# Feeding the second stage earlier: piecewise hand-over of a buffer, twelve row blocks ahead instead of ten, four steps instead of six

## The chip, the cores and the metric

The kernel runs on one core of a Trainium2 chip. The metric is the device time of one execution in microseconds (us), lower is better. The core has five instruction streams that are ordered among each other only by semaphores: PE (matrix multiply, with its weight loads shown as PEld), ACT (activations and copies), DVE (vector work), POOL (vector work without access to the accumulators) and SP, which here issues all the DMAs in one queue.

## What is computed

Two layers follow each other. Layer A is an attention with a recurrent memory: the 2048 rows are cut into 64 segments of 32 rows, and each segment attends to itself and to 8 memory rows that the segment before has produced. So the 64 segments run strictly one after the other. Layer B is a gMLP that mixes all rows, so that its mixing can only begin when the last segment is done.

```python
for s in range(n_seg):                      # layer A, on layernorm(x)
    h = concat([mem, xs[s]])
    q, k, v = (einsum('btd,dhe->bhte', h, W) for W in (Wq, Wk, Wv))
    p = softmax(where(mask, q @ k.T * scale, -1e9))
    o = einsum('bhte,hed->btd', p @ v, Wo)
    mem = o[:, :M]
    outs.append(o[:, M:])
h = x + concat(outs)
...
z  = gelu(layernorm(h) @ w_in)              # layer B, w_in is 512 x 1792
z1 = z[..., :896]
z2 = layernorm(z[..., 896:])
g  = einsum('ts,bsf->btf', w_sp, z2) + b_sp # 2048 x 2048 mixing of the rows
out = h + (z1 * g) @ w_out
```

## The kernel before

All instructions are emitted in program order by hand; each engine runs its own in that order, and a small emitter turns reads and writes of named buffers into semaphore waits (`Emitter.add`, L55). A wait of an instruction holds everything behind it on the same engine.

**The loop over 64 segments** (L916 to L1066). In each segment PE computes Q and K (`QK`, matmul L500), the scores (`S_half`, L538 and L544), V (`V_half`, L591), the column sums of the softmax (`sm_sums`, L559 and L564), the weighted values (`PV_half`, L608 and L614) and the output projection (`Wo`, L641). Between the sums and `PV_half` PE would have to wait for ACT, DVE and POOL to finish the softmax (DVE L579 is its last step for the second half of the heads). This place, called the gap below, is filled with work that doesn't depend on the segment: first with batched work of layer A, one group in each of segments 1 to 47 (`gx`, for example `qkx_mm`, L414, 16 matmuls of 128x128), and then with the first matrix product of layer B for rows that are already final, here called z2 sums (`z2_narrow`, L751). A z2 sum of one row block of 128 rows and one half of 896 columns is 16 narrow matmuls, 4 for each of 4 pieces of the inner dimension; the narrow form (32 stationary columns, four beside each other) keeps the array in the form that the loop uses. A whole group of 16 goes into the gap by `z2_group`. A second supply, `pour`, adds single atoms of 4 narrow matmuls: one in each gap, and one more behind `Wo` in every fourth segment, called the end slot. The atoms are batched V columns (L433) first, and z2 sums after segment 48. The sums are copied out (DVE L759, ACT L761) and stored in DRAM as z2p (L762). In this way 10 of the 16 row blocks (`NP = 10`, L256) have their sums before the loop ends: 15 groups in segments 49 to 63 and 5 from atoms.

**The buffers.** The batched Q and K columns of the memory rows, QTx, lie in two buffers, each for 16 segments; the first half of a buffer holds Q for the 16 segments one after the other, the second half K. At segment s POOL copies its Q part (`qx_copy`, L523), and the matmul L544 reads its K part. The first buffer serves segments 32 to 47 and is free as a whole after them. Then, at segment 47, one DMA loads the second half of w_in into it (`w_in2`, L1059, 896 KB), and one DMA transpose a segment brings the normalised rows of blocks 0 to 7 (`xn2T_dma`, L730; blocks 8 to 10 by L743 into another buffer). The second buffer is free after segment 63; then follow the first half of w_in (`w_in1`, L971) and the transposes of blocks 8 to 13. DMA transposes of w_sp (`wT_piece`, L783 and L784) go through the same queue in every other segment. `z2_back` (L909) brings the stored sums back to the core: blocks 0 to 6 at segment 63, blocks 7 to 9 behind the loop, and the 8 pieces of the transposed w_sp follow them (`load_wT`, L905).

**The second stage** (from L1155). For the row blocks whose sums aren't there yet, 10 to 15, there are six steps k = 0 to 5. Each step has the two z2 sums of its block on PE (`z2_mm`, 4 matmuls L1099 each, then the gelu out of the accumulator, ACT L1102), the gelu of two blocks from DRAM (`z2_gelu`, ACT L1162), the normalisation of these three (`z2_norm`, DVE L1113 and L1115, POOL L1117 and L1119; `z2_apply`, DVE L1124), four groups of z1 (`z1_group`, PE L1131 and ACT L1134), and from k = 2 on the mixing of blocks that are ready into five accumulators (`mix0`, 5 matmuls L1138 for each block). z2 sums, z1 groups and the transposes of the last blocks (`xn2T_pe`, PE L1179, copied by DVE L1094; block 15 at k = 3) take turns on three accumulator banks (`zbank`), so that a matmul waits until the copy out of the third last user of the banks is done. Behind the steps come the remaining z1 groups, the rest of the first mixing, and the other 23 mixings with the output product (L1232).

Of the kernel before, what the change touches and what calls it, by code (L numbers as in the profile page):

```python
# [169 lines left out]
def fast_path(nc, st, keep, A_x, A_mem0, A_Wq, A_Wk, A_Wv, A_Wo, A_seg_len, B_w_in, B_w_sp, B_b_sp, B_w_out, out):  # L170
# [15 lines left out]
    CK = 16  # L186
# [536 lines left out]
    WH = DC * FH  # L723
    w_in2 = region(4 * WSZ, WH).rearrange("p (dc f) -> p dc f", dc=DC)
    w_in1 = region(4 * WSZ + QX, WH).rearrange("p (dc f) -> p dc f", dc=DC)
    xts = [region(4 * WSZ + i * QX + WH, 8 * D).rearrange("p (r dc t) -> p r dc t", r=8, dc=DC) for i in range(2)]
    winr = B_w_in.rearrange("(dc p) f -> p dc f", p=128)

    def xn2T_dma(rb, after):
        sp(lambda e: e.dma_start_transpose(out=xts[rb // 8][:, rb % 8, :, :], in_=xn2_d[rb]), reads=[("xn2d", rb)], writes=[("xn2T", rb)],  # L730
           after=after)
# [4 lines left out]
    def xT2(rb):  # L736
        return xts[rb // 8][:, rb % 8, :, :]

    def xT2z(rb):
        return (hTe[:, rb - 8, :, :], ("xT2e", rb)) if 8 <= rb <= 10 else (xT2(rb), ("xn2T", rb))  # L740

    def xT2e_dma(rb):
        sp(lambda e: e.dma_start_transpose(out=hTe[:, rb - 8, :, :], in_=xn2_d[rb]), reads=[("xn2d", rb)],  # L743
           writes=[("hTe", rb - 8), ("xT2e", rb)])

    def z2_narrow(rb, hf, bank, dcs=range(DC)):
        t, tok = xT2z(rb)
        for dc in dcs:
            for c in range(4):
                q = slice(32 * c, 32 * c + 32)  # L750
                pe(lambda e, dc=dc, q=q, c=c: e.matmul(ps[q, bank, 0:HF], lhsT=t[:, dc, q], rhs=w_in2[:, dc, hf * HF:(hf + 1) * HF],  # L751
                                                       start=(dc == 0), stop=(dc == DC - 1), tile_position=(0, 32 * c)),
                   reads=["w_in2", tok], writes=[PB(bank)])

# [158 lines left out]
    lastop = {}  # L913
    em.mark_const("w_in2")
    zx = [(rb, hf) for rb in range(NP) for hf in range(2)]
    qx_copy(0)  # L916
    for s in range(NSEG):
# [40 lines left out]
        S_half(s, 1)  # L958
        lastop["s"] = em.by_eng["pe"][-1]
        sm_exp(1)  # L960
# [9 lines left out]
        if s == NSEG - 1:  # L970
            sp(lambda e: e.dma_start(w_in1, winr[:, :, 0:FH]), writes=["w_in1"], after=[lastop["s"], lastop["x"]])  # L971
            xn2T_dma(11, [lastop["s"], lastop["x"]])
            z2_back(0, 7, lastop["v"])
        if s + 1 < NSEG:
            qx_copy(s + 1)
            lastop["x"] = em.by_eng["pool"][-1]
        sm_norm(0, pool)
        V_evac(1, "dve")
        sm_norm(1, dve)
        if s == 0:  # L980
# [73 lines left out]
        if j4 == 1 and rb >= 2:  # L1054
            xn2_apply(rb - 2, rb % 2)
            xn2_store(rb - 2, rb % 2)
        if s == 3 * CK - 1:
            free0 = [lastop["s"], px]
            sp(lambda e: e.dma_start(w_in2, winr[:, :, FH:F]), writes=["w_in2"], after=free0)  # L1059
# [17 lines left out]
    NTB = S // TB  # L1077
    em.mark_const("w_in1", "w_out")

# [16 lines left out]
    def z2_mm(rb, hf, bank):  # L1096
        t, tok = xT2z(rb)
        for dc in range(DC):
            pe(lambda e, dc=dc: e.matmul(ps[:, bank, 0:HF], lhsT=t[:, dc, :], rhs=w_in2[:, dc, hf * HF:(hf + 1) * HF],  # L1099
                                         start=(dc == 0), stop=(dc == DC - 1)),  # L1100
               reads=["w_in2", tok], writes=[PB(bank)])
        act(lambda e: e.activation(out=z2[:, rb, hf * HF:(hf + 1) * HF], in_=ps[:, bank, 0:HF], func=ACT.Gelu_apprx_tanh),  # L1102
            reads=[PB(bank)], writes=[("z2", rb, hf)], after=[lastV])

    st2 = sb("st2", [128, 4, 2, 6], F32)
    mv2 = sb("mv2", [128, 4, 2], F32)
    rs2 = sb("rs2", [128, 4], F32)
    nslot = {}

    def z2_norm(rb):  # L1110
        j = nslot[rb] = len(nslot) % 4
        for hf in range(2):
            dve(lambda e, hf=hf: e.bn_stats(out=st2[:, j, hf, :], in_=z2[:, rb, hf * HF:(hf + 1) * HF]), reads=[("z2", rb, hf)],  # L1113
                writes=[("st2", j, hf)])
        dve(lambda e: e.bn_aggr(out=mv2[:, j, :], in_=st2[:, j, :, :].rearrange("p a b -> p (a b)")),  # L1115
            reads=[("st2", j, 0), ("st2", j, 1)], writes=[("mv2", j)])
# [11 lines left out]
    def z1_group(tb, fb, bank):  # L1128
        r0 = 4 * tb
        for dc in range(DC):  # L1130
            pe(lambda e, dc=dc: e.matmul(ps[:, bank, 0:TB], lhsT=w_in1[:, dc, fb * 128:(fb + 1) * 128],  # L1131
                                         rhs=xts[r0 // 8][:, r0 % 8:r0 % 8 + 4, dc, :], start=(dc == 0), stop=(dc == DC - 1)),
               reads=["w_in1"] + [("xn2T", r) for r in range(r0, r0 + 4)], writes=[PB(bank)])
        act(lambda e: e.activation(out=z1T[:, fb, tb * TB:(tb + 1) * TB], in_=ps[:, bank, 0:TB], func=ACT.Gelu_apprx_tanh),  # L1134
# [49 lines left out]
    for k, rb in enumerate(range(NP, RB)):  # L1184
# [853 lines left out]
```

## Time and profile before

| | |
|---|---|
| median of 3 runs | 865.96 us (865.92 to 867.2) |
| the profiled execution, its own time | 866.2 us |
| span of the profiled execution | 864.4 us, so 1.8 us lie around it |
| granted PE clock, mean | 0.999 |
| segment loop | to 700.5 us, where the first L1099 starts |
| second stage up to the first mixing | 700.5 to 719.4 us |
| narrow z2 sums in the loop (L751) | 320 matmuls |
| z2 sums in the second stage (L1099) | 48 matmuls |
| reads of z2p | 1568 KB landed after 9.1 us, 672 KB after 4.4 us |

A line of a timeline shows the start in us from the start of the span, the duration, the engine, the line of the kernel, the operation with what it writes and reads, how many instructions were merged (x16), and in brackets how long the engine was idle before it and what released it. "issue" stands for idle time in which nothing that the profile shows was waited for. SPq is the SP queue issuing a DMA.

### The profile page before, as it was taken

Reading aid. Unit: us, or ns where it says so; the run is one execution under the profiler, and the core shown is the slowest. Engines: PE = TensorE matmul, PEld = TensorE weight load, DVE = VectorE, ACT = ScalarE, POOL = GpSimd, SP = SyncE. Lnnn points to the kernel's source line nnn. Section 1 sums busy time; section 2 is a strip of 40 time slices with the busy share of each in tenths; the row PEclk is TensorE's granted clock in tenths of the full one; section 3 lists DMA queues with packets and bytes.
Section 4 is the critical chain, followed back from the end, with each engine's and each line's share of the span. In section 5 each row is a group of like instructions: output and inputs, shape, how many; then the busy total and the mean of one; then the engine's idle time right before and its main releaser. Section 6 shows DMA issues by size and latency. Waiting matters only on the chain.

```text
span 864.4 us, 45375 instructions
## 1 busy us (share of the span) xinstructions
PE 844.7 (98%) x20839; PEld 476.3 (55%) x20849; DVE 526.8 (61%) x1191; ACT 420.9 (49%) x1085; POOL 158.1 (18%) x404
## 2 busy tenths in 40 slices
PE   6999999999999999999999999899999999999997
PEld 5755555655555655555565555455555544444443
DVE  3455676666666666666767666566666658363443
ACT  2445565555555555555555556455555566400000
POOL 5111122222111212121212121112212114100000
PEclk9999999999999999999999999999999999999999
DMA  9962221313202123121212121623232299032101
GB/s 324 378 216 61 65 60 52 68 31 86 59 25 74 41 59 62 32 65 46 62 37 62 38 60 45 110 70 80 74 64 63 67 241 345 10 109 98 38 13 39
DMA packets 105189, 76.20 MB, mean 88 GB/s; under 512 B 64024, under 2 KB 90528, under 8 KB 104992
## 3 DMA queue, kind: packets, MB, share of 16 engines
q1 hardware_dynamic: 104992, 73.24, 30.8%
q8 instruction: 165, 2.70, 1.4%
q14 instruction: 32, 0.26, 0.1%
HBM read 41.69 MB, written 20.91 MB: 72 GB/s over the span
## 4 chain that ended last, share of the span: by engine, by line
PE 94%; DVE 2%; DMA 1%; SPq 1%; issue 1%; POOL 0%; ACT 0%; DVEq 0%; POOLq 0%
PE f_ps L500 26%; PE f_ps L641 14%; PE f_ps L591 13%; PE f_ps L1138 11%; PE f_ps L414 6%; PE f_ps L692 4%; PE f_ps L1232 3%; PE f_ps L608 2%; PE f_ps L433 2%; PE f_ps L538 2%; PE f_ps L1131 2%; PE f_ps L751 2%; DMA f_arena<-in_A_Wk_dram 1%; PE f_ps L559 1%; DVE f_st L1113 1%; PE f_ps L614 1%
## 5 line engine op out<-in xcount | busy, mean ns | idle before, releaser
L500 PE MATMUL f_ps<-f_arena,f_hT 128*32 128x512 bf16 x4096 | 241.3, 380 | 2.2 <-issue 1.9
L507 ACT ACTIVATE f_Tst<-f_ps 128x512 bf16<-128x512 f32 x256 | 145.9, 596 | 80.5 <-PE f_ps L500 80.3
L500 PEld LDWEIGHTS f_ps<-f_arena,f_hT 128*32 128x32 bf16 x4096 | 94.9, 96 | 104.7 <-ACT f_hT L670 32.5
L591 PE MATMUL f_ps<-f_arena,f_hT 128*32 128x512 bf16 x2048 | 132.9, 378 | 0.0
L641 PE MATMUL f_ps<-f_arena,f_cT 128*32 128x256 bf16 x4096 | 128.6, 273 | 1.1 <-ACT f_cT L627 0.5
L641 PEld LDWEIGHTS f_ps<-f_arena,f_cT 128*32 128x32 bf16 x4096 | 98.2, 96 | 33.6 <-ACT f_cT L627 30.2
L513 DVE STREAM_TRANSPOSE f_QT<-f_Tst 128x256 uint32<-128x256 uint32 x128 | 57.0, 446 | 83.1 <-ACT f_Tst L507 83.1
L600 DVE CAST f_V_sb<-f_ps 128x512 bf16<-128x512 f32 x128 | 88.4, 691 | 29.6 <-PE f_ps L591 29.6
L1138 PE MATMUL f_ps<-f_arena 128*128 128x512 bf16 x448 | 99.6, 379 | 0.0
L523 POOL COPY f_QT<-f_arena 128x256 bf16<-128x256 bf16 x64 | 30.5, 476 | 314.1 <-PE f_ps L544 314.0
L627 ACT ACTIVATE f_cT<-f_ps 128x320 bf16<-128x320 f32 x128 | 49.0, 435 | 56.0 <-PE f_ps L614 56.0
L629 DVE TENSOR_SCALAR f_cT<-f_ps 128x320 bf16<-128x320 f32 x128 | 56.9, 486 | 31.5 <-PE f_ps L614 31.5
L1138 PEld LDWEIGHTS f_ps<-f_arena 128*128 128x128 bf16 x448 | 43.8, 98 | 52.6
L414 PE MATMUL f_ps<-f_hTe,f_arena 128*128 128x128 bf16 x1024 | 66.8, 222 | 2.6 <-DMA f_arena<-in_A_Wq_dram 1.8
L658 DVE CAST f_part<-f_ps 128x256 bf16<-128x256 f32 x64 | 27.2, 425 | 66.0 <-PE f_ps L641 66.0
L414 PEld LDWEIGHTS f_ps<-f_hTe,f_arena 128*128 128x128 bf16 x1024 | 58.9, 99 | 11.7 <-issue 9.6
L591 PEld LDWEIGHTS f_ps<-f_arena,f_hT 128*32 128x32 bf16 x2048 | 45.9, 95 | 27.3 <-issue 0.4
L516 DVE STREAM_TRANSPOSE f_KT<-f_Tst 128x256 uint32<-128x256 uint32 x128 | 55.4, 433 | 8.0
L571 ACT ACTIVATE f_R_sb<-f_ps 128x160 f32<-128x160 f32 x128 | 38.8, 303 | 42.0 <-PE f_ps L564 42.0
L1144 DVE TENSOR_TENSOR f_arena<-f_ps,f_arena 128x512 f32<-128x512 f32 x28 | 19.3, 690 | 60.7 <-PE f_ps L1138 60.7
L670 ACT ACTIVATE f_hT<-f_ps 128x16 bf16<-128x16 f32 x126 | 23.1, 183 | 55.2 <-PE f_ps L665 54.7
L528 DVE CAST f_ps<-f_mask 128x224 f32<-128x224 bf16 x128 | 47.0, 367 | 0.0
(121 smaller groups left out, 1099.8 us busy)
## 6 DMA issues: line engine op xcount, KB each, us to landing
wT_d<-f_wst SPq DMA_DIRECT2D x32, 256.0 KB, 2.4
f_arena<-wT_d SPq DMA_DIRECT2D x32, 256.0 KB, 4.8
f_arena<-in_A_Wq_dram SPq DMA_DIRECT2D x4, 1024.0 KB, 9.0
f_arena<-in_A_Wk_dram SPq DMA_DIRECT2D x4, 1024.0 KB, 14.7
f_arena<-in_A_Wv_dram SPq DMA_DIRECT2D x4, 1024.0 KB, 15.0
f_arena<-in_A_Wo_dram SPq DMA_DIRECT2D x8, 512.0 KB, 9.7
f_Vx<-vext_d SPq DMA_DIRECT2D x63, 64.0 KB, 2.8
vext_d<-f_Vs SPq DMA_DIRECT2D x24, 128.0 KB, 2.1
```

Of the source, the lines that this page charges most:

```text
L414: pe(lambda e, h=h, dc=dc, hh=hh: e.matmul(ps[:, bank, hh * 128:(hh + 1) * 128], lhsT=ws[:, dc, h * DH:(h + 1) * DH], rhs=hTe[:, ck % 3, d ...
L500: pe(lambda e, dc=dc, c=c, rhs=rhs: e.matmul(ps[32 * c:32 * c + 32, bank, :], lhsT=hT[:, sl, dc, :], rhs=rhs, start=(dc == 0), stop=(dc == ...
L507: act(lambda e: e.activation(out=Tst[:, tb, :].rearrange("p (hp i r) -> p hp i r", i=32, r=2), in_=ps[:, bank, :].rearrange("p (hp r i) -> ...
L513: dve(lambda e: e.transpose(out=dst, in_=src), reads=[("T", tb)], writes=[("QT", b)])
L516: dve(lambda e: e.transpose(out=dst, in_=src), reads=[("T", tb)], writes=[("KT", b)])
L528: dve(lambda e: e.tensor_copy(out=ps[:, bank, 0:224], in_=mask[:, :]), reads=["mask"], writes=[PB(bank)])
L591: pe(lambda e, dc=dc, c=c, c0=c0: e.matmul(ps[32 * c:32 * c + 32, bank, :], lhsT=hT[:, sl, dc, :], rhs=w_v[:, dc, c0:c0 + 512], start=(dc ...
L600: dve(lambda e: e.tensor_copy(out=V_sb[:, b, :], in_=ps[:, bank, :]), reads=[PB(bank)], writes=[("V", b)])
L627: act(lambda e: e.activation(out=dst, in_=src, func=ACT.Copy, scale=UNSC), reads=[PB(PVB[c])], writes=[("cT", c)])
L629: dve(lambda e: e.tensor_scalar(out=dst, in0=src, scalar1=UNSC, scalar2=None, op0=ALU.mult), reads=[PB(PVB[c])], writes=[("cT", c)])
L641: pe(lambda e, h=h, g=g, i=i, b=b, c=c: e.matmul(ps[32 * g:32 * g + 32, bank, 0:d1 - d0], lhsT=cTh[:, i, 8:40], rhs=w_o[:, h, d0:d1], star ...
L1138: pe(lambda e: e.matmul(ps[:, bank, 0:TB], lhsT=z2[:, sc, fb * 128:(fb + 1) * 128], rhs=wTb[tb % 2][:, :, sc, :], start=(n == 0), stop=(n ...
```

## The change

QTx's first buffer is handed over piece by piece: each of the four pieces of w_in2 lies in the part of segments that have passed, and so does each row block. The pieces of w_in2 are loaded two at segment 36 and two at segment 39, row blocks 0 to 7 are transposed in at segments 40 to 47 (in the order 0, 4, 1, 5, 2, 6, 3, 7), block 8 at segment 49, 9 to 13 at segments 50, 52, 54, 58 and 62, and w_in1's pieces come at segments 53, 55, 59 and 61, all of them in the second buffer's parts as these become free. With that, z2 sums can be poured from segment 42 on (`Z0`), a whole group goes into the gap from segment 48 on, and in odd segments after 48 `pour` may put two atoms into the gap. The sums of 12 row blocks are made in the loop, 384 narrow matmuls. Laid out by segment, the gaps of 42 to 47 get 4 narrow matmuls more than before (beside 16 of L414), the gap of 48 gets 20 where it had none, those of 49, 51, 53, 57, 59 and 61 get 24 instead of 20, those of 62 and 63 16 instead of 20; the end slots of 44 and 48 get 4, that of 62 none.

The second stage has four steps, for blocks 12 to 15, each with the gelu and the norm of three blocks from DRAM instead of two; the transpose of block 15 moves from k = 3 to k = 2. The line that reads blocks 7 to 11 back stands twice in the new text, one right behind the other, and both issue a DMA. Both write the same buffers, so the second one waits in the SP queue until the first has landed.

```diff
-    NP = 10
+    NP = 12
...
-    w_in2 = region(4 * WSZ, WH).rearrange("p (dc f) -> p dc f", dc=DC)
+    QH = QX // 2
+    w_in2 = [region(4 * WSZ + (dc // 2) * QH + (dc % 2) * FH, FH) for dc in range(DC)]
...
-    xts = [region(4 * WSZ + i * QX + WH, 8 * D).rearrange("p (r dc t) -> p r dc t", r=8, dc=DC) for i in range(2)]
+    xts = [region(4 * WSZ + i * QH + 2 * FH if i < 2 else 4 * WSZ + QX + WH + (i - 2) * 4 * D, 4 * D).rearrange(
+        "p (r dc t) -> p r dc t", r=4, dc=DC) for i in range(4)]
...
+    def load_w_in(half, dc, after):
+        t = (w_in1[:, dc, :], w_in2[dc])[half]
+        tok = ("w_in1", "w_in2")[half]
+        sp(lambda e: e.dma_start(t, winr[:, dc, half * FH:(half + 1) * FH]), writes=[(tok, dc)], after=after)
+        em.mark_const((tok, dc))
...
-    def pour():
-        if s > 3 * CK and not gv.atoms and zx and s + 2 < NSEG:
+    Z0 = 42
+
+    def pour(n=1):
+        if s >= Z0 and not gv.atoms and zx and s + 2 < NSEG:
             z2_atoms()
-        return gv.pour(1 if s else 0)
+        return gv.pour(n if s else 0)
...
-    zx = [(rb, hf) for rb in range(NP) for hf in range(2)]
+    zx = [(rb, hf) for rb in (0, 4, 1, 5, 2, 6, 3, 7, *range(8, NP)) for hf in range(2)]
...
-            sp(lambda e: e.dma_start(w_in1, winr[:, :, 0:FH]), writes=["w_in1"], after=[lastop["s"], lastop["x"]])
-            xn2T_dma(11, [lastop["s"], lastop["x"]])
+            xn2T_dma(8, [xops[s]])
             z2_back(0, 7, lastop["v"])
...
-        late = pour()
-        ev = [] if s == 0 else [gx.pop(0)()] if gx else [z2_group()] if zx and s > 3 * CK else []
+        late = pour(2 if s > 3 * CK and j4 % 2 == 1 else 1)
+        ev = [] if s == 0 else [gx.pop(0)()] if gx else [z2_group()] if zx and s >= 3 * CK else []
...
-        if s == 3 * CK - 1:
-            free0 = [lastop["s"], px]
-            sp(lambda e: e.dma_start(w_in2, winr[:, :, FH:F]), writes=["w_in2"], after=free0)
-        if 0 <= s - 3 * CK + 1 < 8:
-            xn2T_dma(s - 3 * CK + 1, free0)
-        if 8 <= s - 3 * CK + 1 < 11:
-            xT2e_dma(s - 3 * CK + 1)
-        px = lastop.get("x")
-    for r in (12, 13):
-        xn2T_dma(r, [lastop["s"], lastop["x"]])
+        c2, c3 = 2 * CK, 3 * CK
+        if s == c2 + 4:
+            load_w_in(1, 0, [xops[c2 + 3]])
+            load_w_in(1, 2, [sops[c2 + 3]])
+        if s == c2 + 7:
+            load_w_in(1, 1, [xops[c2 + 6]])
+            load_w_in(1, 3, [sops[c2 + 6]])
+        if c2 + 8 <= s < c3:
+            k, m = (s - c2 - 8) // 2, s % 2
+            xn2T_dma(k + 4 * m, [(xops, sops)[m][c2 + 8 + 2 * k]])
+        if s == c3 + 1:
+            xT2e_dma(8)
...
+    z2_back(7, NP, lastop["v"])
     z2_back(7, NP, lastop["v"])
     load_wT(0, [lastop["q"]])
-    for r in (8, 9, 10):
-        xn2T_dma(r, [lastop["s"], lastop["x"]])
...
-        if k == 3:
+        if k == 2:
             xn2T_pe(RB - 1, 1)
-        for r in range(max(0, 2 * k - 2), min(NP, 2 * k)):
+        for r in range(max(0, 3 * k - 3), 3 * k):
             z2_apply(r)
             mixq.append((k, r))
         z2_norm(rb)
...
-        for r in range(2 * k, min(NP, 2 * k + 2)):
+        for r in range(3 * k, 3 * k + 3):
             z2_gelu(r)
             z2_norm(r)
...
-    z2_apply(RB - 1)
-    mixq.append((0, RB - 1))
+    for r in (NP - 3, NP - 2, NP - 1, RB - 1):
+        z2_apply(r)
+        mixq.append((0, r))
```

Left out are the loads of blocks 9 to 13 and of w_in1 in nine segments (placed as told above), the renaming of the buffers in the matmuls, and six instead of four slots for the norm's statistics.

More of the change, by code (lines that the diff above doesn't have):

```diff
@@ L750, in z2_narrow @@
                 q = slice(32 * c, 32 * c + 32)
-                pe(lambda e, dc=dc, q=q, c=c: e.matmul(ps[q, bank, 0:HF], lhsT=t[:, dc, q], rhs=w_in2[:, dc, hf * HF:(hf + 1) * HF],
+                pe(lambda e, dc=dc, q=q, c=c: e.matmul(ps[q, bank, 0:HF], lhsT=t[:, dc, q], rhs=w_in2[dc][:, hf * HF:(hf + 1) * HF],
                                                        start=(dc == 0), stop=(dc == DC - 1), tile_position=(0, 32 * c)),
-                   reads=["w_in2", tok], writes=[PB(bank)])
+                   reads=[("w_in2", dc), tok], writes=[PB(bank)])
     def z2_out(rb, hf, bank, eng):
@@ L913, in fast_path @@
     lastop = {}
-    em.mark_const("w_in2")
-    zx = [(rb, hf) for rb in range(NP) for hf in range(2)]
+    zx = [(rb, hf) for rb in (0, 4, 1, 5, 2, 6, 3, 7, *range(8, NP)) for hf in range(2)]
+    sops, xops = {}, {}
     qx_copy(0)
@@ L958, in fast_path @@
         S_half(s, 1)
-        lastop["s"] = em.by_eng["pe"][-1]
+        lastop["s"] = sops[s] = em.by_eng["pe"][-1]
         sm_exp(1)
@@ L975, in fast_path @@
             qx_copy(s + 1)
-            lastop["x"] = em.by_eng["pool"][-1]
+            lastop["x"] = xops[s + 1] = em.by_eng["pool"][-1]
         sm_norm(0, pool)
@@ L1077, in fast_path @@
     NTB = S // TB
-    em.mark_const("w_in1", "w_out")
+    em.mark_const("w_out")
     def check_stats():
@@ L1098, in z2_mm @@
         for dc in range(DC):
-            pe(lambda e, dc=dc: e.matmul(ps[:, bank, 0:HF], lhsT=t[:, dc, :], rhs=w_in2[:, dc, hf * HF:(hf + 1) * HF],
+            pe(lambda e, dc=dc: e.matmul(ps[:, bank, 0:HF], lhsT=t[:, dc, :], rhs=w_in2[dc][:, hf * HF:(hf + 1) * HF],
                                          start=(dc == 0), stop=(dc == DC - 1)),
-               reads=["w_in2", tok], writes=[PB(bank)])
+               reads=[("w_in2", dc), tok], writes=[PB(bank)])
         act(lambda e: e.activation(out=z2[:, rb, hf * HF:(hf + 1) * HF], in_=ps[:, bank, 0:HF], func=ACT.Gelu_apprx_tanh),
             reads=[PB(bank)], writes=[("z2", rb, hf)], after=[lastV])
-    st2 = sb("st2", [128, 4, 2, 6], F32)
-    mv2 = sb("mv2", [128, 4, 2], F32)
-    rs2 = sb("rs2", [128, 4], F32)
+    NR = 6
+    st2 = sb("st2", [128, NR, 2, 6], F32)
+    mv2 = sb("mv2", [128, NR, 2], F32)
+    rs2 = sb("rs2", [128, NR], F32)
     nslot = {}
     def z2_norm(rb):
-        j = nslot[rb] = len(nslot) % 4
+        j = nslot[rb] = len(nslot) % NR
         for hf in range(2):
@@ L1131, in z1_group @@
             pe(lambda e, dc=dc: e.matmul(ps[:, bank, 0:TB], lhsT=w_in1[:, dc, fb * 128:(fb + 1) * 128],
-                                         rhs=xts[r0 // 8][:, r0 % 8:r0 % 8 + 4, dc, :], start=(dc == 0), stop=(dc == DC - 1)),
-               reads=["w_in1"] + [("xn2T", r) for r in range(r0, r0 + 4)], writes=[PB(bank)])
+                                         rhs=xts[tb][:, :, dc, :], start=(dc == 0), stop=(dc == DC - 1)),
+               reads=[("w_in1", dc)] + [("xn2T", r) for r in range(r0, r0 + 4)], writes=[PB(bank)])
         act(lambda e: e.activation(out=z1T[:, fb, tb * TB:(tb + 1) * TB], in_=ps[:, bank, 0:TB], func=ACT.Gelu_apprx_tanh),
```

16 lines of the change are left out of this document (11 added, 5 removed).

## The prediction

> **What bounds the kernel now.** First the page: the busy times and the chain that ended last.
>
> ```profile
> PE 844.7 (98%) x20839; PEld 476.3 (55%) x20849; DVE 526.8 (61%) x1191; ACT 420.9 (49%) x1085; POOL 158.1 (18%) x404
> ...
> PE 94%; DVE 2%; DMA 1%; SPq 1%; issue 1%; POOL 0%; ACT 0%; DVEq 0%; POOLq 0%
> ```
>
> PE has 98% of the span and 94% of the chain. Work that only moves from one place of PE to another gains nothing, except where it lands in time that PE spends waiting. So there are three questions: what a matmul costs in the gap, what PE waits for in the second stage, and whether a wait goes elsewhere.
>
> The timeline of POOL gives the length of a segment, since L523 runs once in each.
>
> ```profile
> 449.00 0.48 POOL L523 COPY f_QT<-f_arena 128x256 bf16<-128x256 bf16 x1 [6.49 <-PE f_ps L544]
> 459.25 0.48 POOL L523 COPY f_QT<-f_arena 128x256 bf16<-128x256 bf16 x1 [2.44 <-PE f_ps L544]
> 500.97 0.47 POOL L523 COPY f_QT<-f_arena 128x256 bf16<-128x256 bf16 x1 [2.44 <-PE f_ps L544]
> 511.05 0.47 POOL L523 COPY f_QT<-f_arena 128x256 bf16<-128x256 bf16 x1 [3.16 <-PE f_ps L544]
> 541.30 0.47 POOL L523 COPY f_QT<-f_arena 128x256 bf16<-128x256 bf16 x1 [2.44 <-PE f_ps L544]
> 553.61 0.48 POOL L523 COPY f_QT<-f_arena 128x256 bf16<-128x256 bf16 x1 [3.20 <-PE f_ps L544]
> 563.69 0.48 POOL L523 COPY f_QT<-f_arena 128x256 bf16<-128x256 bf16 x1 [6.49 <-PE f_ps L544]
> ```
>
> A segment with an atom and 16 of L414 in its gap takes 10.25 us (449.00 to 459.25), one with the 16 alone 10.08 (500.97 to 511.05), one with 20 narrow z2 matmuls 10.08 too (553.61 to 563.69). One segment takes 12.31, 2.23 too many (541.30 to 553.61); more on it below.
>
> **The gap.** Two gaps in PE's timeline, and for the second the DVE step that its second half waits for:
>
> ```profile
> 377.78 0.20 PE L564 MATMUL f_ps<-f_E_sb,f_ones 128*32 128x64 bf16 x4
> 377.81 0.39 PE L433 MATMUL f_ps<-f_arena,f_hTe 128*32 128x512 bf16 x4
> ...
> 379.13 0.27 PE L608 MATMUL f_ps<-f_E_sb,f_V_sb 32*128 32x40 bf16 x16
> ...
> 379.28 0.27 PE L608 MATMUL f_ps<-f_E_sb,f_V_sb 32*128 32x40 bf16 x15
> ```
>
> ```profile
> 574.24 0.20 PE L564 MATMUL f_ps<-f_E_sb,f_ones 128*32 128x64 bf16 x4
> 574.27 1.12 PE L751 MATMUL f_ps<-f_arena 128*32 128x448 bf16 x20
> 575.32 0.27 PE L608 MATMUL f_ps<-f_E_sb,f_V_sb 32*128 32x40 bf16 x16
> ...
> 575.59 0.28 PE L608 MATMUL f_ps<-f_E_sb,f_V_sb 32*128 32x40 bf16 x16
> ...
> 575.20 0.33 DVE L579 TENSOR_TENSOR f_E_sb<-f_R_sb,f_E_sb 128x160 bf16<-128x160 f32 x1
> ```
>
> From L564 to the second L608 it is 1.35 us with 20 narrow ones, and 1.50 with 4 narrow ones of 512 columns and the 16 of L414 behind them. In the second gap DVE ends at 575.53 and the second L608 starts 0.06 later: up to here the filler is free, and 16 of L414 alone are as free, by the equal 10.08. Beyond it PE is late, by 0.15 to 0.17 (1.50 less 1.35, 10.25 less 10.08).
>
> Segments 42 to 47 get 4 narrow ones of 448 columns beside the 16: 0.16 x 448/512 = 0.14 each, six times **+0.84**. The narrow ones follow each other in (575.32 - 574.27)/20 = 0.0525 us, so a fourth set is at most 0.21 (six: 1.26), and nothing if the softmax hides it. The six gaps with 24: PE's first L608 then comes at 574.27 + 24 x 0.0525 = 575.53, the second 0.15 later as in the first gap, 575.68 instead of 575.59: six times 0.09, **+0.54** (ends 0 and 1.26). I take the values between, since the row with 16 and 4 shows that most of an atom gets through. Segment 48 gets 20 where there was nothing: free, like the other gaps of 20. Segments 62 and 63 lose an atom and gain nothing by it, for the same reason. The end slots are free too: the stretch of 500.97 has the empty one of segment 44 in it, the stretch of 553.61 that of 49 with four matmuls of `F_group`, and both take 10.08 (one slot more in all; at most 0.21). The copies out, one more on DVE and three on ACT, fall to engines that have 61% and 49% of the span. In sum **+1.4** for the loop, from 0 to 2.5.
>
> **The stall at 547 us.** In the segment of 12.31 us:
>
> ```profile
> 538.28 0.40 SPq L1059 DMA_DIRECT2D f_arena<-in_B_w_in_dram  x1
> ```
>
> ```profile
> 549.06 1.26 PE L500 MATMUL f_ps<-f_arena,f_hT 128*32 128x512 bf16 x20 [1.90 <-issue]
> ```
>
> ```profile
> 547.00:548.00 1.00, 0.16 (x3) 0.00 (x0) 0.00 (x0) 0.00 (x0) 0.00 (x0) 1.00 2.23 44
> ```
>
> PE stands for 1.90 us in the middle of a block of equal matmuls, with no releaser ("issue"), while the DMA queues are full (the last column but one is the DMA share, 2.23 of the engines' time): the 896 KB of w_in2 were issued at 538.28, and transposes follow them in the queue. I read it as instructions that came late because their fetch stood behind the burst. The transposes that follow in later segments do no such harm: 553.61 to 563.69 is 10.08 with one of them. The change loads w_in2 in pieces of 224 KB, two at a time, eight and eleven segments earlier. Value: **-2.2**, ends -2.2 and +1 (another place with two transposes behind each other stalls).
>
> The Trainium skill ("Runtime: NRT & Kernel Launch", section "Instruction fetch mechanics") says that the sequencer fetches the next 16 KiB block over a DMA queue of its own while it runs the current one, and that crossing a block is "mostly hidden". By that the 1.90 us are no late fetch and the smaller pieces bring nothing: 869.4 rather than 867.2. The trace has the 1.90 us under "issue" and shows no other releaser.
>
> **The second stage.** Now PE, ACT and DVE in the steps k = 1 to 3 of before.
>
> ```profile
> 710.18 3.78 PE L1131 MATMUL f_ps<-f_arena 128*128 128x512 bf16 x16
> 713.80 1.68 PE L1099 MATMUL f_ps<-f_arena 128*128 128x448 bf16 x8
> 715.31 1.03 PE L1131 MATMUL f_ps<-f_arena 128*128 128x512 bf16 x4
> 716.76 2.76 PE L1131 MATMUL f_ps<-f_arena 128*128 128x512 bf16 x12 [0.42 <-ACT f_arena L1102]
> 719.36 3.40 PE L1138 MATMUL f_ps<-f_arena 128*128 128x512 bf16 x15
> ...
> 724.11 0.39 PE L1179 MATMUL f_ps<-f_ident,f_xo 128*128 128x128 bf16 x4
> 724.34 1.89 PE L1131 MATMUL f_ps<-f_arena 128*128 128x512 bf16 x8
> 726.39 1.90 PE L1131 MATMUL f_ps<-f_arena 128*128 128x512 bf16 x8 [0.17 <-DVE f_arena L1094]
> ```
>
> ```profile
> 714.49 1.78 ACT L1162 ACTIVATE f_arena<-f_arena 128x896 bf16<-128x896 bf16 x2
> 716.17 0.97 ACT L1102 ACTIVATE f_arena<-f_ps 128x448 bf16<-128x448 f32 x2
> ```
>
> ```profile
> 715.81 1.15 DVE L1113 BATCH_NORM_STATS2 f_st<-f_arena 128x6 f32<-128x448 bf16 x2
> ...
> 719.93 0.21 DVE L1115 BATCH_NORM_AGGREGATE f_mv<-f_st 128x2 f32<-128x12 f32 x1
> ...
> 725.97 0.37 DVE L1094 COPY f_arena<-f_ps 128x512 bf16<-128x512 bf16 x1
> ```
>
> Two steps less take away 16 of L1099; 8 last 1.51 us (713.80 to 715.31): **-3.02**. (They cost 1.05 x 64/20 = 3.4 in the loop, but there they lie in waits, as above.)
>
> But PE is stopped between the steps. Three banks rotate; the second z1 group of a step needs the bank of the first z2 sum, which ACT copies out behind the two L1162 of the step before. At 716.17 a z1 group was due (715.31 + 4 x 0.215); it came at 716.76, 0.59 late. With three L1162, 0.89 more each:
> - Into k = 1: there the 16 matmuls from 710.18 took 3.62 to the next start instead of 16 x 0.216 = 3.46, 0.16 late; now 0.16 + 0.89 = **1.05** late. k = 2 starts at 713.80 + 0.89 = 714.69.
> - Into k = 2: ACT begins the three L1162 at 714.49 + 0.89 = 715.38 and needs 2.67, and the bank is free at about 718.5 (before 716.7, 2.2 after the start of two). The transposes of block 15 now stand between, so already the first z1 group needs this bank; it was due at 714.69 + 1.51 + 0.23 = 716.43: **2.06** late.
> - The third z1 group then needs the bank of the transposes, which DVE copies (L1094) behind the norms of step 1. A norm takes DVE 1.25 (1.15 of L1113 and about half of L1115, before the next begins). With one more in step 0, the queue of step 1 reaches its first norm at 715.81 + 1.25 = 717.06; from there to the last norm's end it took 719.93 + 0.21 - 715.81 = 4.33 with two blocks from DRAM, now about 5.6: 722.7. With the copy of 0.37 PE goes on at 723.05; due 718.49 + 2 x 0.86 = 720.21: **2.84** late.
>
> At k = 3 four blocks of mixing (20 x 0.216 = 4.3) stand before it, and both engines have caught up. Before, the same places had 0.16 + 0.59 + 0.33 (726.39 less 724.34 is 2.05 for two groups of 0.86) = 1.08. So the stage costs 5.95 - 1.08 - 3.02 = **+1.85**. If DVE is no hindrance, it is 1.85 - 2.84 + 0.33 = -0.7; if each engine is a third later than worked out, 1.85 + 2 = 3.8.
>
> **The doubled read.** The queue behind the loop, and what the reads take to land (the last column, us):
>
> ```profile
> 701.86 0.53 SPq L762 DMA_DIRECT2D z2p_d<-f_Vs  x1
> ...
> 707.76 0.38 SPq L909 DMA_DIRECT2D f_arena<-z2p_d  x1
> 708.18 4.44 SPq L905 DMA_DIRECT2D f_arena<-wT_d  x8
> ```
>
> ```profile
> f_arena<-wT_d SPq DMA_DIRECT2D x32, 256.0 KB, 4.8
> ...
> f_arena<-z2p_d SPq DMA_DIRECT2D x1, 1568.0 KB, 9.1
> ...
> f_arena<-z2p_d SPq DMA_DIRECT2D x1, 672.0 KB, 4.4
> ```
>
> Before, the read waited for the last store, which landed 5.9 us after its issue (701.86 to 707.76). The atoms' last store is gone, so the read of blocks 7 to 11 can start between 702 and 705.4. It is 1120 KB, 6.7 us between the two rows, and the second one waits for it: 709 to 712. The last piece of w_sp is issued 4.9 later and lands 4.8 after that, at 718.7 to 721.7, or at 723.5 if the second read's 6.7 stand ahead of it. The first mixing is due at 723.05 + 1.74 (two z1 groups) = 724.8. So the doubled read and what queues behind it (w_sp, then b_sp, w_out and h) cost **nothing**, covered by PE's own stalls; without these PE would be there at about 719.7 and wait up to 4 us.
>
> **The sum.** The profiled execution took 866.2 (span 864.4 and 1.8 around it; the median of the runs shown is 865.96). 866.2 + 1.4 - 2.2 + 1.85 = **867.2**. About 0.2%, 1.7 us, is what a measurement of this kernel tells from no change, so this is within it, on the slow side.
>
> **The rivals.**
> - *The stall at 547 us stays or comes elsewhere* (chance 0.22): 866.2 + 1.4 + 1.85 = 869.4, slower. For it: nine transposes move to segments that had none, straight in front of those of w_sp; against it: the later segments with such pairs take 10.08.
> - *The steps have no longer stalls than before* (0.08): the stage keeps its -3.02, so 866.2 + 1.4 - 2.2 - 3.0 = 862.4, faster. It needs ACT and DVE to be through a step 1 to 3 us earlier than their rows say; against it stand the 0.59 and 0.33 that two blocks a step already cost.
> - *The doubled read holds w_sp* (0.10): it decides when the last piece lands later than 724.8. With the late end of each landing (723.5) and 2 to 5 us more in a full queue it is 867.2 + 1 to 4, about 870, slower.
> - *DVE's copy comes in time, ACT doesn't* (0.10): the stage is -0.7, so 866.2 + 1.4 - 2.2 - 0.7 = 864.7, and less if the gaps take some atoms for nothing.
> - *The forecast* (0.50): 865.5 to 868.5 by its own terms.
>
> Slower by over 0.2% (above 867.7): 0.22 + 0.10 + 0.12 of the forecast's own width = 0.44. Faster (below 864.2): 0.08 + 0.04 + 0.03 = 0.15. Within: 0.41. The range from 864.4 to 870.0 leaves out the 862.4 and the far end of the doubled read, and holds the bounds of the other terms.
>
> **What would show it.** In the new profile: L523 10.2 apart in segments 42 to 47 and 10.1 to 10.2 in odd ones after 48; no segment of over 11 us near 541; PE idle before L1131 from ACT L1102 about 1 and 2 us, then from DVE L1094 about 2.5; the first L1138 some 24 us behind the first L1099 (18.8 before), without a DMA as releaser. A stall of 2 us under "issue", a first L1138 released by w_sp, or z1 groups that follow each other without idle time in k = 1 and 2 would prove me wrong.

## The result, and the profile after

| | before | after |
|---|---|---|
| median, same comparison | 865.18 us (864.16 to 867.2, 12 runs) | 867.99 us (866.82 to 870.28, 12 runs) |
| ratio after/before, 95% interval | | 1.0028 [1.0014, 1.0041] |
| profiled execution, span | 866.2, 864.4 us | 867.64, 865.7 us |
| start of the first z2 sum of the second stage | 700.53 | 700.03 |
| from there to the first mixing | 18.83 | 24.24 |
| from there to the end of the span | 163.87 | 165.67 |

By the ratio the changed kernel is slower by 0.28%, that is 2.4 us of 865.2, between 1.2 and 3.5; the ratio is not the quotient of the two medians, which lie 2.8 us apart. In the profiles the loop ends 0.5 us earlier, and the second stage lasts 1.80 us longer although it has two steps less. The busy times of the page of after:

```profile
span 865.7 us, 45493 instructions
...
PE 844.1 (98%) x20897; PEld 474.0 (55%) x20897; DVE 527.1 (61%) x1192; ACT 421.8 (49%) x1086; POOL 157.9 (18%) x404
```

PE is as busy as before, so the difference lies in where it waits. The segments first, by POOL's copy in the timeline of after (one copy in each segment):

```profile
480.91 0.48 POOL L523 COPY f_QT<-f_arena 128x256 bf16<-128x256 bf16 x1 [6.57 <-PE f_ps L544]
491.72 0.47 POOL L523 COPY f_QT<-f_arena 128x256 bf16<-128x256 bf16 x1 [7.06 <-PE f_ps L544]
501.94 0.48 POOL L523 COPY f_QT<-f_arena 128x256 bf16<-128x256 bf16 x1 [2.44 <-PE f_ps L544]
...
542.98 0.48 POOL L523 COPY f_QT<-f_arena 128x256 bf16<-128x256 bf16 x1 [2.49 <-PE f_ps L544]
553.07 0.47 POOL L523 COPY f_QT<-f_arena 128x256 bf16<-128x256 bf16 x1 [3.17 <-PE f_ps L544]
```

A segment with an early atom takes 10.22 us (491.72 to 501.94; 10.08 before). The place at 547 us, where before has a segment of 12.31, takes 10.09 (542.98 to 553.07). A shorter stall stays elsewhere: 480.91 to 491.72 is 10.81 us. Before has one at that place too, 11.20 us long, with PE idle under "issue" for 0.75; its two copies, and the row of PE:

```profile
479.69 0.48 POOL L523 COPY f_QT<-f_arena 128x256 bf16<-128x256 bf16 x1 [6.49 <-PE f_ps L544]
490.89 0.48 POOL L523 COPY f_QT<-f_arena 128x256 bf16<-128x256 bf16 x1 [6.71 <-PE f_ps L544]
```

```profile
482.51 0.20 PE L608 MATMUL f_ps<-f_E_sb,f_V_sb 32*128 32x40 bf16 x3 [0.75 <-issue]
```

The second stage, in PE's timeline of after; the brackets hold PE's idle time ahead of a row and what ended it:

```profile
708.16 1.69 PE L1115 MATMUL f_ps<-f_arena 128*128 128x448 bf16 x8
709.68 1.03 PE L1148 MATMUL f_ps<-f_arena 128*128 128x512 bf16 x4
711.53 2.76 PE L1148 MATMUL f_ps<-f_arena 128*128 128x512 bf16 x12 [0.82 <-ACT f_arena L1118]
714.13 1.68 PE L1115 MATMUL f_ps<-f_arena 128*128 128x448 bf16 x8
715.64 0.39 PE L1196 MATMUL f_ps<-f_ident,f_xo 128*128 128x128 bf16 x4
717.93 1.90 PE L1148 MATMUL f_ps<-f_arena 128*128 128x512 bf16 x8 [1.90 <-ACT f_arena L1118]
722.53 1.90 PE L1148 MATMUL f_ps<-f_arena 128*128 128x512 bf16 x8 [2.70 <-DVE f_arena L1110]
724.27 4.48 PE L1155 MATMUL f_ps<-f_arena 128*128 128x512 bf16 x20
```

These are the three holds that the prediction worked out as 1.05, 2.06 and 2.84 us late, in its order and from its engines: 0.82 and 1.90 for ACT's copy of a z2 sum behind three gelus, 2.70 for DVE's copy of block 15. The brackets give idle time; as lateness, counted the prediction's way from these rows, the three are 0.99, 2.06 and 2.88 us. Each hold is PE waiting for one of three accumulator banks. What keeps ACT and DVE, in their timelines of after:

```profile
714.83 2.62 ACT L1179 ACTIVATE f_arena<-f_arena 128x896 bf16<-128x896 bf16 x3
717.34 0.97 ACT L1118 ACTIVATE f_arena<-f_ps 128x448 bf16<-128x448 f32 x2
```

```profile
716.60 1.15 DVE L1130 BATCH_NORM_STATS2 f_st<-f_arena 128x6 f32<-128x448 bf16 x2
...
721.98 0.21 DVE L1132 BATCH_NORM_AGGREGATE f_mv<-f_st 128x2 f32<-128x12 f32 x1
722.10 0.37 DVE L1110 COPY f_arena<-f_ps 128x512 bf16<-128x512 bf16 x1
```

The copy starts at 722.10, behind four norms that began at 716.60. It was forecast for 722.7 with the loop's end of before; from the first z2 sum that is 22.17 us, and 22.07 were measured. Last, the queue with the doubled read, and the row for the last two of the first eight transposed pieces of w_sp:

```profile
706.36 5.92 SPq L919 DMA_DIRECT2D f_arena<-z2p_d  x2
712.33 4.30 SPq L915 DMA_DIRECT2D f_arena<-wT_d  x8
```

```profile
L915 SPq DMA_DIRECT2D f_arena<-wT_d x2: 439/476/514, 715.6 to 716.2; - x2
...
DMA to landing us min/median/max: 7.6/7.7/7.8
```

The two reads take the queue from 706.36 to 712.3. The last piece of w_sp is issued at 716.2 and lands at most 7.8 later, at 724.0; the first mixing starts at 724.27. No DMA is named as its releaser, but only about 0.3 us were left.

### The profile page after: what moved, and what is told of

It is laid out like the page before. It is cut to its first block, busy times and chain, and to the rows that moved or that the text cites. A ratio compares the mean times of both kernels' runs of the same rounds, so it can differ in the third digit from the quotient of the medians.

```text
span 865.7 us, 45493 instructions
## 1 busy us (share of the span) xinstructions
PE 844.1 (98%) x20897; PEld 474.0 (55%) x20897; DVE 527.1 (61%) x1192; ACT 421.8 (49%) x1086; POOL 157.9 (18%) x404
## 4 chain that ended last, share of the span: by engine, by line
PE 95%; DVE 2%; POOL 1%; issue 1%; DMA 0%; ACT 0%; DVEq 0%; POOLq 0%
PE f_ps L500 26%; PE f_ps L641 14%; PE f_ps L591 13%; PE f_ps L1155 11%; PE f_ps L414 6%; PE f_ps L692 4%; PE f_ps L1250 3%; PE f_ps L608 2%; PE f_ps L433 2%; PE f_ps L1148 2%; PE f_ps L759 2%; PE f_ps L538 2%; PE f_ps L559 1%; DVE f_st L1130 1%; PE f_ps L439 1%; PE f_ps L614 1%
## 5 line engine op out<-in xcount | busy, mean ns | idle before, releaser
L414 PE MATMUL f_ps<-f_hTe,f_arena 128*128 128x128 bf16 x1024 | 66.4, 222 | 2.8 <-DMA f_arena<-in_A_Wq_dram 1.5
L414 PEld LDWEIGHTS f_ps<-f_hTe,f_arena 128*128 128x128 bf16 x1024 | 58.7, 99 | 12.5 <-issue 8.6
L649 POOL COPY f_cTx<-f_cT 128x256 bf16<-128x256 bf16 x64 | 25.4, 396 | 118.8 <-DVE f_cT L629 118.8
```

The lines of the kernel that those rows point to most:

```text
L414: pe(lambda e, h=h, dc=dc, hh=hh: e.matmul(ps[:, bank, hh * 128:(hh + 1) * 128], lhsT=ws[:, dc, h * DH:(h + 1) * DH], rhs=hTe[:, ck % 3, d ...
```

## The experiments

Each was compared with the kernel before on its own chip; ratios are against that, with 95% intervals, and a gain in us is worked out from the ratio. The distances of the copies and the stage times are from the profile of each run. First what the same kernel gives against itself.

**g4, before unchanged.**

> The kernel before, unchanged, once more against itself: how far two medians of the same kernel lie apart (expected: within 0.2%, so 863.5 to 867), and whether its profile shows the 12.31 us between the two copies around 547 us and the 1.90 us without a named cause at L500 again. Theory, that the single load of w_in2 sets that stall: it is there again, with 1.5 us or more. Rival, that it is a hold of one execution which falls anywhere: the distance there is 10.1 to 10.5 us and the longest distances stand elsewhere.

Measured: 865.02 us, ratio 0.9993 [0.9982, 1.0005]; so about 0.1% is the distance of two equal kernels. Its profile has the stall at the same instruction, shorter: PE's timeline of g4, and the two copies around it.

```profile
548.21 2.97 PE L500 MATMUL f_ps<-f_arena,f_hT 128*32 128x512 bf16 x49 [0.81 <-issue]
```

```profile
541.55 0.48 POOL L523 COPY f_QT<-f_arena 128x256 bf16<-128x256 bf16 x1 [2.44 <-PE f_ps L544]
552.76 0.48 POOL L523 COPY f_QT<-f_arena 128x256 bf16<-128x256 bf16 x1 [3.12 <-PE f_ps L544]
```

The distance is 11.21 us, 1.13 more than 10.08, where the profile before had 2.23 more. The stall belongs to this place of the kernel; its length changes from execution to execution, and the 0.81 is short of the 1.5 that was expected. That it came here in before by chance is out. The other place repeats as well, with 10.97 us and the same 0.75 under "issue".

**g3 and h3, the hand-over alone** (the split loads of w_in2, but ten blocks poured from segment 49 on, and the second stage of before).

```diff
-    NP = 12
+    NP = 10
...
-    Z0 = 42
+    Z0 = 3 * CK + 1
...
-        late = pour(2 if s > 3 * CK and j4 % 2 == 1 else 1)
+        late = pour()
...
```

> The hand-over of the Q/K columns and the four split loads alone: ten poured blocks from segment 49 on in the order of before, one unit a segment, the second stage of before (six steps, one read, transposes of block 15 in step 4). No gap of segments 42 to 48 carries a z2 sum. Theory, that the split loads save a stall of TensorE which the gaps then eat: e4 took 0.3 less than before with 1.3 of gaps, so a saving of 1.6 and, without the early gaps, 863.6 here. Rival, that the 1.90 us stall belongs to the one profiled execution and the split loads save nothing in the median: 865.2, equal to before within 0.2%. In between (about 864.4) neither would be settled.

> The hand-over alone once more, for comparison on the same chip: 0.998 of before by g3. If it comes out at 1.000, what g3 showed was scatter of the medians.

Measured: 864.15 us, ratio 0.9978 [0.9963, 0.9994], and 864.07 us, ratio 0.9981 [0.9970, 0.9993]. The segment at 547 us takes 10.47 and 10.08. The hand-over saves 1.6 to 1.9 us (0.0019 and 0.0022 of 865), and 1.3 against g4, the kernel before beside it on the same chip (0.9978 to 0.9993); the rival of no saving lies outside both intervals. Not all of it belongs to the stall at 547 us. The segment of 11.20 and 10.97 us at 480 us takes 10.10 and 10.36 with the hand-over, so in the profiles a second stall, on which the prediction has no term, gives up 0.6 to 1.1.

**h1, the load of before cut in two.**

```diff
-            sp(lambda e: e.dma_start(w_in2, winr[:, :, FH:F]), writes=["w_in2"], after=free0)
+            sp(lambda e: e.dma_start(w_in2[:, 0:2, :], winr[:, 0:2, FH:F]), writes=["w_in2"], after=free0)
+        if s == 3 * CK:
+            sp(lambda e: e.dma_start(w_in2[:, 2:4, :], winr[:, 2:4, FH:F]), writes=[("w_in2", 1)], after=free0)
...
```

> The kernel before, with its one load of w_in2 (896 KB in segment 47) cut into two of 448 KB, one in segment 47 and one in 48; nothing else moves. Theory, that TensorE's instructions come late behind the bytes of one burst: the distance of the copies around 547 us, 12.31 and 11.21 us in the two profiles of before, falls to 10.1 to 10.5, no time under issue at L500 there, and the median lies 1 to 2 below before, near the hand-over alone (ratio about 0.998). Rival, that the place in the program or the transposes next to the load set the stall, not the size of the burst: a distance of 11 us or more stays at 547 or shows one segment later, ratio 1.000.

**h2, the hand-over with the bytes put back** (896 KB loaded a second time in segment 47, in four DMAs).

```diff
+        if s == c3 - 1:
+            for dc in range(DC):
+                load_w_in(1, dc, [sops[s]])
```

> The hand-over alone (g3), with the four pieces of w_in2 loaded once more, 896 KB in one go in segment 47, the same bytes into the same place, so that nothing in the result changes. Theory of the burst: the stall is back at the 547 us place (distance of the copies 11 us or more, g3 had 10.47), and the time is 1 to 2 above the hand-over alone. Rival: the distance stays at 10.5 or below and the time equals that of the hand-over alone within 0.2%.

Measured: h1 864.23 us, ratio 0.9986 [0.9975, 0.9997], the segment at 547 us 10.08 and the next one 10.45. Cutting the load takes most of the stall away, as the burst theory wanted, and gains 1.2 us rather than 2; the segment at 480 us still takes 11.20. h2: 864.56 us, ratio 0.9984 [0.9968, 1.0000], the segment 10.40; 896 KB in four DMAs don't bring the stall back. They were issued from 541.12 to 543.26, some 3 us later than the load of before, so h2 leaves open whether the cut or the later start spares PE. The theory holds for the one large DMA at its place, not for the bytes as such. What goes with the length of the stall is in the DMA view. Its rows by queue, for 538.6 to 545.3 us, are these of before and these of h1:

```profile
q1 hardware_dynamic: 1316, 1.12, 106.5%
q14 instruction: 2, 0.02, 3.2%
```

```profile
q1 hardware_dynamic: 1795, 1.25, 79.4%
q8 instruction: 1, 0.02, 1.5%
q14 instruction: 2, 0.02, 1.2%
```

q8 is a queue of instruction packets of 16 KB, usually some 4 us apart. In before none came in these 6.7 us, in h1 one did, though more bytes moved. From the start times of the packets in the traces, the distance of the two around 541 us, beside the excess of that segment over 10.08:

| run | two packets of q8 apart, us | excess, us |
|---|---|---|
| before | 8.10 | 2.23 |
| g4 | 7.45 | 1.13 |
| g3 | 6.68 | 0.39 |
| h2 | 6.56 | 0.32 |
| h3 | 5.66 | 0.00 |
| h1 | 5.47 | 0.00 |
| e2 (below) | 5.45 | 0.28 |

From 6.56 on the excess grows with the distance; below that it is nothing or, in e2, as small as the 0.32 of h2. The end of a packet says more. In before the late packet came from 546.60 to 547.65; PE had stopped at 547.16 and went on at 549.06, 1.4 us behind the packet's end. After the first 20 us the thirteen profiles have 34 places where PE stands under "issue" for 0.2 us or more, the 0.75 at 482.51 among them, and at every one PE goes on 1.30 to 1.64 us behind the end of a packet of q8. With packets some 4 us apart, chance would put about one place in twelve into these 0.34 us. So PE was waiting for instructions. What delays a packet stays open. The late one of before took 1.05 us itself, no longer than its neighbours, so it began late; no run delayed a packet alone, and g3 has 6.68 without any load there.

**e4, the loop alone** (hand-over and early pouring with ten blocks, the six steps of before, one read). Its diff against after:

```diff
-    NP = 12
+    NP = 10
...
-    z2_back(7, NP, lastop["v"])
...
-        if k == 2:
+        if k == 3:
             xn2T_pe(RB - 1, 1)
-        for r in range(max(0, 3 * k - 3), 3 * k):
+        for r in range(max(0, 2 * k - 2), min(NP, 2 * k)):
...
```

> The hand-over by pieces and the earlier pouring alone: 10 row blocks and six steps as before, one read. The stage is then as before (first mixing 18.8 us behind its first z2 sum). Theory of the prediction: the gaps with an atom more cost 6 x 0.15 + 5 x 0.09 = 1.3 us, and the stall of 2.2 us is gone, so 0.9 us less than the kernel before, 864.3. Rival (the stall of the profiled execution is not one that most executions have; the median doesn't gain by its going): 1.3 us more, 866.5, 1.0015 of the kernel before.

Measured: 864.95 us, ratio 0.9994 [0.9982, 1.0007]; the 0.999 of the theory lies inside the interval, the 1.0015 of the rival outside. Against g3 and h3 (0.9978, 0.9981) the early pouring costs 0.0013 to 0.0016, that is 1.1 to 1.4 us: what was forecast for the gaps, though from different comparisons, whose intervals are as wide as the cost. In sum the loop saves about half a microsecond.

**e1, one read; e2, block 15's transposes back at k = 3; e3, both.**

```diff
-    z2_back(7, NP, lastop["v"])
     z2_back(7, NP, lastop["v"])
```

```diff
-        if k == 2:
+        if k == 3:
             xn2T_pe(RB - 1, 1)
```

> The changed kernel with the read of blocks 7 to 11 issued once. Theory (the doubled read is covered by PE's stops in the second stage): no change against the changed kernel, about 868.0 us and 1.003 of the kernel before; the first L1155 still 24.2 us behind the first z2 sum of the stage, held by DVE's copy of block 15. Rival (the second read holds w_sp and so the first mixing): about 3 us less, 865.

> The changed kernel with the transposes of block 15 back at k = 3. Theory (DVE's copy and w_sp's last piece end within 0.3 us of each other, 724.3 and 724.0 in the profile of after): the idle time before z1 from DVE (2.7 us) goes, and a wait of about 3 us for w_sp appears ahead of the first mixing, so about 867.7, hardly less than the changed kernel. Rival (DVE's copy alone sets the end, as the prediction has it): about 3.4 us less, 864.6, 0.999 of the kernel before.

> The changed kernel with both: the transposes of block 15 at k = 3 and one read. Theory: now neither holds the first mixing; it comes 20.8 to 21.1 us behind the stage's first z2 sum instead of 24.2, and the time is 3.0 to 3.4 us less than the changed kernel, 864.6 to 865.0, 0.999 to 1.000 of the kernel before. Rival (the cost lies in the loop, in late instructions or in the added atoms): no change, 868.

| | median, us | ratio [95%] | first z2 sum to first mixing | to the end of the span |
|---|---|---|---|---|
| after | 867.99 | 1.0028 [1.0014, 1.0041] | 24.24 | 165.67 |
| e1 | 868.51 | 1.0032 [1.0015, 1.0049] | 24.24 | 165.85 |
| e2 | 867.44 | 1.0017 [1.0000, 1.0034] | 23.38 | 164.91 |
| e3 | 865.10 | 0.9994 [0.9981, 1.0007] | 20.50 | 164.03 |

Without the second read alone nothing changes; without the hold for DVE's copy alone, little; without both, 0.0034, or 2.9 us. On their own chip e3 lies 0.0038 below e1 and 0.0023 below e2, so it takes both, and the rival of a cost in the loop is out. In the profiled stage the pattern is the same, but smaller: +0.18, -0.76 and -1.64 us for e1, e2 and e3 against after. Two causes that each cover the other. PE's timeline of e1, where DVE's copy still holds PE for as long:

```profile
720.85 1.90 PE L1147 MATMUL f_ps<-f_arena 128*128 128x512 bf16 x8 [2.70 <-DVE f_arena L1109]
```

Of e2, where that hold is gone and w_sp is the releaser in its place:

```profile
718.69 2.76 PE L1148 MATMUL f_ps<-f_arena 128*128 128x512 bf16 x12 [1.26 <-ACT f_arena L1118]
...
724.17 1.02 PE L1155 MATMUL f_ps<-f_arena 128*128 128x512 bf16 x4 [2.71 <-DMA f_arena<-wT_d]
```

And of e3, where three shorter holds are left:

```profile
710.47 2.76 PE L1147 MATMUL f_ps<-f_arena 128*128 128x512 bf16 x12 [0.82 <-ACT f_arena L1117]
...
716.87 2.76 PE L1147 MATMUL f_ps<-f_arena 128*128 128x512 bf16 x12 [1.26 <-ACT f_arena L1117]
...
728.75 1.90 PE L1147 MATMUL f_ps<-f_arena 128*128 128x512 bf16 x8 [1.33 <-DVE f_arena L1109]
```

The three holds sum to 3.41 us: the four steps with one read keep back the 3.02 that two steps less should bring.

**g1, a version without these holds.** Twelve blocks poured, one read, two, two, three and five of them in the four steps, block 15's transposes between the z1 groups of step 3, and eight slots for the norm's statistics. Against e3, without the slots and the last loop:

```diff
+    cut = (0, 2, 4, 7, 12)
...
-        if k == 3:
-            xn2T_pe(RB - 1, 1)
-        for r in range(max(0, 3 * k - 3), 3 * k):
+        for r in range(cut[k - 1] if k else 0, cut[k]):
...
-            z1_some(4)
+            z1_some(2)
+            if k == 3:
+                xn2T_pe(RB - 1, 1)
+            z1_some(2)
-        for r in range(3 * k, 3 * k + 3):
+        for r in range(cut[k], cut[k + 1]):
```

> The changed kernel with one read of the last five z2 sums, two, two, three and five poured blocks in the four steps, eight slots for their statistics, and block 15's transposes in step 3 between the second and the third z1 group. Theory, that nothing but the holds for a PSUM bank sets the second stage: the same changed kernel with three blocks a step and the transposes at the head of step 3 took 865.10 and its TensorE was held 0.82, 1.26 and 1.33 us there; with two blocks in steps 0 and 1 the ten-block run was held 0.42 us in the same places, and behind two more z1 groups block 15's copy keeps no bank from anybody. So 865.10 - (0.82 + 1.26 + 1.33 - 0.42) = 862.1, with the first mixing 18.8 us behind the first z2 sum, as in that ten-block run. Rival, that VectorE and ScalarE only run late by as much further on, with three and five blocks in steps 2 and 3: about 864.5 to 865, and new waits for DVE or ACT at a z1 or mixing row behind step 2.

Measured: 862.19 us, ratio 0.9955 [0.9940, 0.9971], faster than both kernels. The first mixing comes 18.97 us behind the first z2 sum, and the stage lasts 160.95. PE's timeline of g1:

```profile
716.48 2.76 PE L1147 MATMUL f_ps<-f_arena 128*128 128x512 bf16 x12 [0.42 <-ACT f_arena L1117]
719.22 3.40 PE L1154 MATMUL f_ps<-f_arena 128*128 128x512 bf16 x15
```

Only the 0.42 is left of the holds, and PE has no other wait of 0.2 us from there to the end of the span: the rival of 864.5 is out.

**g2, g1 with the second read.**

```diff
+    z2_back(7, NP, lastop["v"])
     z2_back(7, NP, lastop["v"])
```

> The kernel of g1 with the second read of the last five z2 sums put back, and nothing else. Theory, that the doubled read holds the w_sp pieces back: in the changed kernel they landed at 724.0, 24.0 us behind the first z2 sum, where the first mixing of this kernel wants them 18.8 us behind; so a wait for a DMA of about 5.1 us at the first mixing and 862.1 + 5.1 = 867.2. Rival, as the prediction had it (last piece landed at 718.7 to 723.5, so 18.7 to 23.5 us behind the first z2 sum, and a read that costs nothing in its lower half): 862.1 to 863, no wait for a DMA there.

Measured: 869.05 us, ratio 1.0039 [1.0026, 1.0052]; against g1 0.0084, or 7.3 us. PE's timeline of g2, the row for the last pieces of w_sp, and a table of two stretches (the last column but two is the granted clock):

```profile
722.99 5.62 PE L1155 MATMUL f_ps<-f_arena 128*128 128x512 bf16 x15 [5.28 <-DVE f_mv L1132]
```

```profile
L915 SPq DMA_DIRECT2D f_arena<-wT_d x2: 432/892/1353, 714.6 to 716.0; - x2
...
DMA to landing us min/median/max: 6.9/7.2/7.6
```

```profile
718.00:722.90 4.90, 0.00 (x0) 0.00 (x0) 4.03 (x12) 2.86 (x4) 1.89 (x5) 0.77 1.05 393
722.99:725.00 2.01, 2.01 (x5) 0.70 (x6) 1.98 (x5) 0.00 (x0) 1.40 (x4) 0.50 1.06 390
```

The last piece lands at 716.0 + 6.9 = 722.9, and PE goes on at 722.99. The row names DVE L1132, whose result this matmul doesn't read; the landing is what fits. The wait is the expectation's 5.1 (5.28). But 867.2 was expected: the 2.2 beyond the wait are the mixing itself, where 15 matmuls take 5.62 us instead of g1's 3.40, for the most part at a granted clock of 0.50.

## Why the prediction was right, point by point

The predicted 867.2 lies 0.8 below the measured 867.99, which is inside the range and 0.3 above the 867.7 from which the text called it slower. Part of that closeness is luck. As a change the sum says +1.05 from 866.2, and +2.4 were measured; it was the high base, 1.0 above the median, that brought 867.2 near. The mechanisms are another matter. The terms:

| term | forecast | measured |
|---|---|---|
| gaps | +1.4 | +1.1 to +1.4 (e4 against g3 and h3) |
| stall at 547 us | -2.2 | -1.6 to -1.9 for the hand-over (g3, h3), a second stall included; -1.2 for cutting the load (h1) |
| second stage | +1.85 | +1.80 in the profiles |
| doubled read | 0 | 0 (e1), with 0.3 us to spare |

- **Gaps: right.** With the gaps of 42 to 47 a segment takes 10.21 to 10.31 for 10.08, but for the one with the 10.81; with 24 narrow matmuls it takes 10.16 or 10.17, the 0.09 of the prediction, but for one of 10.56 where before has 10.28.
- **The stall: late instructions are shown, that they stood behind the burst is not; too large in its size.** I took the 2.2 of one profiled execution for the term. The second profile of before shows 1.1, cutting the load gains 1.2, and the 1.6 to 1.9 of the hand-over take in the stall at 480 us, which I had not seen. In after 0.59 of that one is left. For the same reason the base was high: the profiled 866.2 lies 1.0 above the median of 865.18. The two errors go against each other in the sum. The page of the Trainium skill that the prediction weighed ("Runtime: NRT & Kernel Launch", section "Instruction fetch mechanics") has the fetch "mostly hidden"; in the profile of before the waits behind late packets of 0.2 us and more come to 3.0 us of 864, one of them 1.90.
- **The second stage: right, step by step.** The lateness was 0.99, 2.06 and 2.88 us for 1.05, 2.06 and 2.84, in sum 5.93 for 5.95, and the engines were the right ones. The first mixing came 24.24 us behind the first z2 sum, for "some 24".
- **The doubled read: right in its price, too low in its landing.** I let the last of these pieces of w_sp land at 718.7 to 723.5; it was 724.0, though the loop ended 0.5 earlier. The read began at 706.36, not between 702 and 705.4, since a store of z2 sums ahead of it, issued at 698.98, took 7.4 us to land; and a piece took up to 7.8 us instead of 4.8. I called its cover "PE's own stalls", and e2 shows that cover taken away: 2.71 us of waiting for w_sp. The "up to 4 us" without these stalls were 5.28 in g2.
- **The rivals.** The stall at 547 us didn't stay (10.09) and none as long came elsewhere, the holds grew, and DVE's copy didn't come in time (2.70). The rival of w_sp held back missed by 0.3 us: it decides as soon as PE is earlier, as e2 and g2 show.
- **Left open.** Against the median of before the three terms give +1.4 - 1.8 + 1.8 = 1.4 us, and 2.4 were measured, between 1.2 and 3.5, so the sum is just inside. By the ratios after lies 2.9 above e4 and e1 3.3 above e3 (0.0034 and 0.0038), while their profiled stages are longer by 1.2 and 1.8 only. If that is more than scatter, a microsecond or so of the slowdown is in no profile taken here. The granted clock of the single executions hints at where: its mean is 0.997 in eight of the twelve of after and four of the twelve of e1, and never below 0.998 in e3 and e4; of the 35 of before on e1's chip four lie at 0.997 or lower. The profiled executions of after and e1 have 0.999, and that of e1 took 866.15, 2.4 less than e1's median. So in many executions the clock may have dropped somewhere; no profile here shows it.

## What to carry to other kernels

Where engines hand banks round in turn, work taken off the busiest engine can come back as its waits: move the copy that frees a bank to where nobody waits for it, and spread what stands before it, as g1 does, before you count the saved matmuls. Two delays that end at the same time hide each other, so take both away together before you call either harmless. A stall of one profiled execution needs a second profile before its length becomes a term of a sum.

## What the chip showed beside this

- In the 5.28 us without a matmul (g2, from 717.71 on) the granted clock fell to 0.50 at about 720.7, and it came back at 727.5, 4.5 us after the work had begun again; the median mixing matmul at 0.50 took 631 ns, where it takes 379 in g1; the wait and the slower matmuls together cost 5.28 + 2.2 = 7.5 us, and g2 is 7.43 longer than g1 from the first z2 sum to the end (168.38 and 160.95). Behind the 2.70 us of after and the 2.71 of e2 the clock stayed at 1.00. The Trainium skill ("TensorE: Matmul & The Clock Gate", section "Part 1: The HAM clock gate") has the array fall to half rate after an idle window of about 3.4 us, and back after about as much work; the trace agrees roughly, with a fall 3.0 us into the wait and a return 4.5 us into the work, and with none at 2.71.
- The first eight 256 KB pieces of w_sp took 6.0 to 7.8 us to land in after and 6.9 to 7.6 in g2, but 5.8 to 7.5 in e1 as well, with one read; in before they took 4.4 to 5.7. So the second read is not what made the single piece slower; what did, no run shows.
- Wherever PE stood under "issue" for 0.2 us or more after the first 20 us, in 34 places of twelve profiles (e4 has none), it went on 1.30 to 1.64 us behind the end of a 16 KB instruction packet of q8.
- Beside one DMA of 896 KB the instruction packets of q8 came 7.5 to 8.1 us apart, beside two of 448 KB in two segments 5.5, beside the same bytes as four DMAs, 3 us later, 6.6, and with no load there 5.7 and 6.7.
